# An attention backward kernel: dV and dK accumulated transposed with 512-column moving operands, and four turns per head given to the crossbar

## The chip, the cores and the metric

One core of a Trainium2 chip. The metric is the device time of one execution in microseconds, as the median of several runs. All runs used here were in the same, undisturbed state (one core has no second state to be confused with, and no run was more than 1.5% above the fastest of its kernel).

PE is TensorE (its weight loads are listed as PEld), DVE is VectorE, ACT is ScalarE, POOL is GpSimd, SP is SyncE. SP issues all the crossbar transposes, POOL issues the plain loads and stores of the attention.

## The reference, cut to what matters

The whole computation is a forward pass and its gradient. The part that the change touches is the gradient of 32 attention heads, each with S = 2048 queries and keys and a head size of 128:

```python
q = (x @ wq).reshape(B, Sq, H, Dh).transpose(0, 2, 1, 3)          # H = 32, Dh = 128, Sq = Sk = 2048
p = softmax(einsum("bhqd,bhkd->bhqk", q, k_cache) * Dh ** -0.5)
o = einsum("bhqk,bhkd->bhqd", p, v_cache)
...
# what jax.vjp asks for in each head, with dO the gradient of o:
#   dV = P^T dO          dP = dO V^T        dS = P * (dP - rowsum(P * dP)) * Dh ** -0.5
#   dK = dS^T Q          dQ = dS K
```

The weights' gradients and the gated branch come before and after this; the change does not touch them. All tensors are bf16.

## The kernel before

A matmul here contracts over the 128 partitions. `lhsT` is the loaded weight (128 columns at most), `rhs` is the moving operand (up to 512 columns), and the result goes to PSUM.

Each head has 16 "P slots" (scores, exponentials, transposed probabilities P^T, O) and then 16 "dS slots" (dP, dS, dS^T, dQ). One slot is one block of 128 queries. The slab of a slot, `Pq`, is 128 queries by 2048 keys, 512 KB; dS later overwrites P in it. The crossbar turns each slab, so there are 32 turns per head, and each is used five slots after it was asked for:

```python
skew = min(SKEW if fast else 2, NT // 2)      # SKEW = 5, NT = 16
def transpose_slab(hs, qt, name):             # P^T and dS^T, 512 KB each
    T = wpt.tile([P, NT, P], bf, name=name, tag="PT")          # a ring of 7 buffers
    nc.sync.dma_start_transpose(T[:], hs.slabs[qt][:])
    return T
def tail_part(hs, T, rhs, part):              # O from P^T and V, dQ from dS^T and K
    if part == 0:
        hs.acc = acc_tile()
    for kt in range(part * NT // 2, (part + 1) * NT // 2):
        nc.tensor.matmul(hs.acc[:, 0, :], lhsT=T[:, kt, :], rhs=rhs[:, kt, :], start=(kt == 0), stop=(kt == NT - 1))
```

The scores need K^T and dP needs V^T. Those were made by PE, 16 transposes of 128 columns each per head, with copies out of PSUM by ACT or DVE:

```python
def prep_kt(hs):
    KTv = hs.KT[:].rearrange("p (t q) -> p t q", q=P)
    pe_transpose_blocks(lambda j: hs.Kn[:, j, :], 0, NT, lambda g, n: KTv[:, g:g + n, :], "s")
def prep_vt(hs): ...                          # the same for V, copies by DVE
```

dV and dK were accumulated in their stored layout, in two halves of eight slabs each. Here the slab is the weight and dO or Q (128 columns) moves:

```python
class Partial:                                # [...] __init__ cut
    def step(self):
        kt = self.kt
        j = kt % 4
        if j == 0:
            self.tile = acc_tile()
        for qt in range(self.lo, self.hi):
            nc.tensor.matmul(self.tile[:, j, :], lhsT=self.slabs[qt][:, kt * P:(kt + 1) * P], rhs=self.rhs[:, qt, :],
                             start=(qt == self.lo), stop=(qt == self.hi - 1))
        self.kt += 1
        if j == 3 or self.kt == NT:
            # [...] first half: copy to the fp32 tile `part`; second half:
            fo_ = stg.tile([P, 4, P], bf, name="kvo", bufs=4)
            nc.vector.scalar_tensor_tensor(fo_[...], self.tile[...], self.factor, self.part[...], op0=ALU.mult, op1=ALU.add)
            nc.gpsimd.dma_start(self.out_dram.rearrange("(p t) d -> p t d", t=NT)[:, k0:kt + 1, :], fo_[:, :j + 1, :])   # 128 KB
```

A plan says in which slot each side task stands (b1 is the head's first P slot, b2 its first dS slot, pl the head before's first dS slot):

```python
for c in range(4):
    put(pl + q(c), 0, lambda c=c: load_k(hd(), c, 4))                # K in four loads of 128 KB
    put(pl + q(skew + 3 + c), 0, lambda c=c: load_v(hd(), c, 4))     # V too
put(pl + q(skew + 3), NT * P, lambda: prep_kt(hd()))
# [...]
put(b1 + q(NSC + 2), NT * P, lambda: prep_vt(hd()))
# [...]
spread(b1 + NTH, lambda: first("v", hd().dOn, 0, NTH, "v"))          # dV, first half
spread(b2, lambda: Partial(hd(), NTH, NT, hd().dOn, parts["v"], out_3[0, h], None))
spread(b2 + NTH, lambda: first("k", hd().Qn, 0, NTH, "s", SCALE))    # dK
spread(b2 + NT, lambda: Partial(hd(), NTH, NT, hd().Qn, parts["k"], out_2[0, h], None, SCALE))
```

## Time and profile before

| | before |
|---|---|
| time, median of 3 runs | 5019.34 us (5018.45 to 5020.46) |
| span of the profiled run, mean granted PE clock | 5024.2 us, 0.997 |
| attention (first scores to the last head's dQ and dK) | 3134 us, so about 98 us per head |

The page of the kernel before: the busy time of each engine with its share of the span, the granted PE clock and the busy share of the DMA engines in 40 slices (tenths), and the chain that ended last.

```profile
PE 4914.6 (98%) x53584; PEld 3475.1 (69%) x54480; DVE 2582.2 (51%) x6721; ACT 2575.9 (51%) x4637; POOL 961.8 (19%) x1507
...
PEclk9999999999999999999999999999999999999999
DMA  7887999999999999999999999999996665797876
...
PE 92%; DMA 3%; issue 3%; DVE 1%; ACT 0%; SPq 0%; POOL 0%; POOLq 0%; ACTq 0%; DVEq 0%
```

PE is the bound: it is busy nearly all the time, at full clock, and the chain is PE.

The costliest groups of the kernel before that the change touches: line, engine, operation, output and inputs, shapes, count, then busy us and the mean ns of one, then the idle time of PE just before them and what ended most of it. L737 is dV and dK, L677 is O and dQ, L146 is the transposes of K and V.

```profile
L737 PE MATMUL acc<-dOn,Pq 128*128 128x128 bf16 x8192 | 552.3, 219 | 10.1
L677 PE MATMUL acc<-Kn,dST 128*128 128x128 bf16 x8192 | 551.3, 219 | 9.1 <-DMA dST<-Pq 5.5
L677 PE MATMUL acc<-Vn,PT 128*128 128x128 bf16 x8192 | 547.4, 219 | 17.0 <-DMA PT<-Pq 10.1
...
L737 PE MATMUL acc<-Qn,Pq 128*128 128x128 bf16 x8192 | 540.6, 219 | 3.4
...
L146 PE MATMUL acct<-ident,Vn 128*128 128x128 bf16 x512 | 34.1, 219 | 0.0
L146 PE MATMUL acct<-ident,Kn 128*128 128x128 bf16 x496 | 32.7, 219 | 1.6
```

The mean of 219 ns is the length of one matmul in a pipeline where several overlap; what PE pays is the distance from start to start. The PE timeline shows it (start, length, line, tiles, count):

```profile
2005.03 1.50 PE L737 MATMUL acc<-dOn,Pq 128*128 128x128 bf16 x24
2006.37 0.59 PE L700 MATMUL dp<-VT,dOT 128*128 128x512 bf16 x2
2006.80 1.06 PE L677 MATMUL acc<-Kn,dST 128*128 128x128 bf16 x16
2007.70 0.59 PE L700 MATMUL dp<-VT,dOT 128*128 128x512 bf16 x2
```

Sixteen matmuls of 128 columns take 2007.70 − 2006.80 = 0.90 us to the start of the next group, so 56 ns each; two of 512 take 0.43 us, so 216 ns each. Taken over all starts, the pitches are 55.83 and 215.8 ns. This agrees with the Trainium skill, TensorE: Matmul & The Clock Gate, section "Back-to-back issue gap", whose formula, given there for an isolated matmul, comes to 55.8 and 215.8 ns. A matmul of 512 columns costs 3.87 of 128, not 4: that is all that wider moving operands can save.

Of some forms of 512 columns the trace before lacks records (4718 of 5376 in the attention are there, while the code asks for the full number), so counts of these are taken from the code, and PE's busy time before is somewhat too low.

Three stretches of the kernel before in the windows view (start and end in us, length, busy us and count of PE, PEld, DVE, ACT, POOL, then the granted PE clock, the DMA share, which counts overlapping packets and so can pass 1, and GB/s):

```profile
1000.00:3000.00 2000.00, 1978.28 (x25515) 1593.24 (x25924) 1282.88 (x3370) 1370.72 (x2294) 352.34 (x575) 1.00 1.09 210
2068.00:2088.00 20.00, 19.74 (x270) 16.44 (x273) 15.04 (x64) 15.19 (x28) 1.51 (x2) 1.00 1.25 234
2052.00:2062.00 10.00, 9.89 (x143) 8.47 (x142) 5.54 (x21) 7.77 (x15) 4.03 (x8) 1.00 1.05 173
```

PE is 98.9% busy at full clock in the long stretch.

### The profile page before, as it was taken

To read this page: it belongs to the slowest core of one execution; us is meant where nothing else is said; L and a number is where in the kernel's file an instruction comes from. 1 tells how busy PE (TensorE), PEld (TensorE's weight loads), DVE (VectorE), ACT (ScalarE), POOL (GpSimd) and SP (SyncE) were. 2 spreads that over 40 slices of the span, in tenths; PEclk is the share of its full clock that TensorE was granted. 3 is DMA by queue.
4 is the path that set the end of the run, shared out by engine and by line. 5 is a ranking of instruction groups with operands and counts; after the bars stand their busy time and mean duration, and the time that the engine had idled before them with its cause. 6 is when DMAs were issued, how large, how long until landed. Compare 5 with 4: busy or idle time off the path is not lost.

```text
span 5024.2 us, 128236 instructions
## 1 busy us (share of the span) xinstructions
PE 4914.6 (98%) x53584; PEld 3475.1 (69%) x54480; DVE 2582.2 (51%) x6721; ACT 2575.9 (51%) x4637; POOL 961.8 (19%) x1507
## 2 busy tenths in 40 slices
PE   9999999999999999999999999999889999999999
PEld 4445787787787788778778877877646666555554
DVE  4545666666666666666666666665425444200111
ACT  5422766766666676666667666666413333211000
POOL 3322111111111111111111111111222222211000
PEclk9999999999999999999999999999999999999999
DMA  7887999999999999999999999999996665797876
GB/s 260 273 206 167 211 213 205 206 215 212 202 214 216 201 212 208 214 208 209 215 202 213 206 213 210 209 215 203 209 196 206 195 189 183 223 264 178 171 140 121
DMA packets 2762803, 1031.39 MB, mean 205 GB/s; under 512 B 2665377, under 2 KB 2669602, under 8 KB 2762210
## 3 DMA queue, kind: packets, MB, share of 16 engines
q1 hardware_dynamic: 2659746, 699.38, 75.7%
q0 software_dynamic: 101856, 323.05, 20.0%
q8 instruction: 428, 7.01, 0.6%
q14 instruction: 165, 1.35, 0.1%
q10 hardware_dynamic: 608, 0.59, 0.0%
HBM read 175.31 MB, written 182.13 MB: 71 GB/s over the span
## 4 chain that ended last, share of the span: by engine, by line
PE 92%; DMA 3%; issue 3%; DVE 1%; ACT 0%; SPq 0%; POOL 0%; POOLq 0%; ACTq 0%; DVEq 0%
PE acc L737 18%; PE acc L677 18%; PE acc L975 13%; PE sp L630 8%; PE dp L700 7%; PE acc L1157 6%; PE acc L213 6%; PE u_ps L448 3%; PE g_ps L446 3%; PE dh L1036 3%; PE acc L531 3%; PE acct L146 2%; PE acc L945 2%; DMA dST<-Pq 1%; DMA xnT<-on_d 1%
## 5 line engine op out<-in xcount | busy, mean ns | idle before, releaser
L648 ACT ACTIVATE Pq<-sp 128x1024 bf16<-128x1024 f32 x1024 | 1048.1, 1024 | 309.7 <-PE sp L630 196.4
L737 PEld LDWEIGHTS <-Pq 128*128 128x128 bf16 x16384 | 1003.9, 98 | 244.3 <-issue 1.1
L703 DVE SCALAR_TENSOR_TENSOR Pq<-dp,negdelta,Pq 128x1024 bf16<-128x1024 f32 x512 | 655.3, 1280 | 37.7 <-PE acc L677 36.5
L706 ACT ACTIVATE t<-dp,negdelta 128x1024 bf16<-128x1024 f32 x512 | 568.1, 1116 | 178.4 <-PE dp L700 123.0
L677 PEld LDWEIGHTS <-PT 128*128 128x128 bf16 x8192 | 501.0, 98 | 128.6 <-DMA PT<-Pq 11.5
L677 PE MATMUL acc<-Vn,PT 128*128 128x128 bf16 x8192 | 547.4, 219 | 17.0 <-DMA PT<-Pq 10.1
L737 PE MATMUL acc<-dOn,Pq 128*128 128x128 bf16 x8192 | 552.3, 219 | 10.1
L677 PE MATMUL acc<-Kn,dST 128*128 128x128 bf16 x8192 | 551.3, 219 | 9.1 <-DMA dST<-Pq 5.5
L630 PE MATMUL sp<-KQ 128*128 128x512 bf16 x1762 | 547.1, 379 | 2.2 <-ACT Pq L648 2.1
L737 PE MATMUL acc<-Qn,Pq 128*128 128x128 bf16 x8192 | 540.6, 219 | 3.4
L700 PE MATMUL dp<-VT,dOT 128*128 128x512 bf16 x1728 | 540.8, 379 | 0.0
L707 DVE TENSOR_TENSOR Pq<-t,Pq 128x1024 bf16<-128x1024 bf16 x512 | 354.6, 693 | 359.7 <-ACT t L706 351.9
L677 PEld LDWEIGHTS <-dST 128*128 128x128 bf16 x8192 | 492.0, 98 | 68.2 <-DMA dST<-Pq 7.4
L718 ACT ACTIVATE dq_n<-acc,rsc 128x128 bf16<-128x128 f32 x512 | 188.4, 368 | 331.7 <-PE acc L677 329.4
L1174 DVE SCALAR_TENSOR_TENSOR junk<-acc,xn_all 128x512 f32<-128x512 f32 (+1 forms) x32 | 13.9, 453 | 635.6 <-ACT dxn L1173 635.6
L751 POOL DMA_DIRECT2D out_dram<-kvo x256 | 140.8, 550 | 999.7 <-DVE kvo L749 999.7
L671 POOL DMA_DIRECT2D on_d<-o_n x128 | 97.3, 760 | 721.4 <-DVE junk L689 374.8
L1038 DVE TENSOR_TENSOR du_blk<-dh,ah 128x256 bf16<-128x256 f32 x288 | 120.4, 419 | 195.5 <-PE dh L1036 193.4
L1173 ACT ACTIVATE dxn<-acc 128x512 f32<-128x512 f32 (+1 forms) x32 | 12.8, 407 | 396.7 <-PE acc L1157 389.2
L635 DVE TENSOR_REDUCE rs_all<-rsp 128x1 f32<-128x2 f32 x512 | 78.1, 153 | 255.7 <-ACT Pq L648 253.4
L50 DVE TENSOR_SCALAR o_n<-acc,rinv_all 128x128 bf16<-128x128 f32 x352 | 123.3, 350 | 161.5 <-PE acc L677 161.5
L648 ACT ACTIVATION_READ_ACCUMULATOR Pq<-sp 128x1 f32 x1024 | 200.5, 196 | 0.0
(213 smaller groups left out, 6977.0 us busy)
## 6 DMA issues: line engine op xcount, KB each, us to landing
out_dram<-kvo POOLq DMA_DIRECT2D x256, 128.0 KB, 4.2
ah<-a_d POOLq DMA_DIRECT2D x18, 1024.0 KB, 7.2
ah<-h_d POOLq DMA_DIRECT2D x18, 1024.0 KB, 9.4
du_d<-du_blk POOLq DMA_DIRECT2D x18, 1024.0 KB, 8.0
dg_d<-dg_blk POOLq DMA_DIRECT2D x18, 1024.0 KB, 9.7
h_d<-h_row POOLq DMA_DIRECT2D x64, 256.0 KB, 3.5
a_d<-a_row POOLq DMA_DIRECT2D x64, 256.0 KB, 3.7
x_all<-in_A_k_cache_dram SPq DMA_DIRECT2D x64, 256.0 KB, 3.8
```

What stands on the lines that cost most here:

```text
L213: nc.tensor.matmul(av[:, :CH], lhsT=w[:, i, :], rhs=srcT[:, i, cs], start=(i == 0), stop=(i == DT - 1))
L630: nc.tensor.matmul(sp[:, c * CH:(c + 1) * CH], lhsT=hs.QT[:, qt * P:(qt + 1) * P], rhs=hs.KT[:, hf * HW_ + c * CH: hf * HW_ + (c + 1) * CH ...
L648: nc.scalar.activation(Pq[:, hsl], sp[:], AF.Exp, scale=SCALE, accum_out=hs.rsp[:, hf:hf + 1])
L677: nc.tensor.matmul(hs.acc[:, 0, :], lhsT=T[:, kt, :], rhs=rhs[:, kt, :], start=(kt == 0), stop=(kt == NT - 1))
L700: nc.tensor.matmul(dp[:, c * CH:(c + 1) * CH], lhsT=hs.dOT[:, qt * P:(qt + 1) * P], rhs=hs.VT[:, hf * HW_ + c * CH: hf * HW_ + (c + 1) * C ...
L703: nc.vector.scalar_tensor_tensor(Pq[:, hsl], dp[:], hs.negdelta[:, qt:qt + 1], Pq[:, hsl], op0=ALU.add, op1=ALU.mult)
L706: nc.scalar.activation(t[:], dp[:], AF.Identity, bias=hs.negdelta[:, qt:qt + 1], scale=1.0)
L707: nc.vector.tensor_tensor(Pq[:, hsl], t[:], Pq[:, hsl], op=ALU.mult)
L718: nc.scalar.activation(hs.dq_n[:, qt % G4, :], hs.acc[:, 0, :], AF.Copy, scale=hs.rsc[:, qt:qt + 1])
L737: nc.tensor.matmul(self.tile[:, j, :], lhsT=self.slabs[qt][:, kt * P:(kt + 1) * P], rhs=self.rhs[:, qt, :], start=(qt == self.lo), stop=(q ...
L975: nc.tensor.matmul(accs[j][:, :nn], lhsT=lhs[:, st, cols], rhs=rhs[:, st, n0:n0 + nn], start=(st == 0), stop=(st == NT - 1))
L1157: nc.tensor.matmul(self.accs[sl][j][:, :nn], lhsT=ch[:, kk, sl * P:(sl + 1) * P], rhs=wT[:, k0 + kk, n0:n0 + nn], start=(self.k + kk == 0) ...
```

## The change

Intent: give dV and dK the cheaper form, with `nat` (dO or Q) as the weight and the slab moving, 512 columns at a time. The result is dV^T or dK^T, so it is written as bf16 into a tile that is free at that time (the head's K^T or V^T), turned by the crossbar, and stored in one transfer of 512 KB. And take the transposes of K and V off PE: the crossbar turns the loaded K and V.

```diff
+            def turn_nat(dst, src):
+                nc.sync.dma_start_transpose(dst[:].rearrange("p (t q) -> p t q", q=P), src[:].rearrange("p t d -> p (t d)"))
...
             class Partial:
                 def step(self):
-                    for qt in range(self.lo, self.hi):
-                        nc.tensor.matmul(self.tile[:, j, :], lhsT=self.slabs[qt][:, kt * P:(kt + 1) * P], rhs=self.rhs[:, qt, :],
+                    chunk, j = divmod(self.n, SUB)
+                    cs = slice(chunk * CH, (chunk + 1) * CH)                      # CH = 512, SUB = 4
+                    for qt in range(self.lo + m * j // SUB, self.lo + m * (j + 1) // SUB):
+                        nc.tensor.matmul(self.acc, lhsT=self.nat[:, qt, :], rhs=self.slabs[qt][:, cs],
                                          start=(qt == self.lo), stop=(qt == self.hi - 1))
...
-                            nc.gpsimd.dma_start(self.out_dram.rearrange("(p t) d -> p t d", t=NT)[:, k0:kt + 1, :], fo_[:, :j + 1, :])
+                    nc.vector.scalar_tensor_tensor(self.turned[:, cs], self.acc, self.factor, self.part[:, cs], op0=ALU.mult, op1=ALU.add)
+                    if chunk == NCH - 1:
+                        kvn = stg.tile([P, NT, P], bf, name="kvn", bufs=1)
+                        nc.sync.dma_start_transpose(kvn[:], self.turned)
+                        nc.gpsimd.dma_start(self.out_dram.rearrange("(p t) d -> p t d", t=NT), kvn[:])
...
-                    put(pl + q(skew + 3), NT * P, lambda: prep_kt(hd()))
+                    put(pl + q(NTH + 3), 0, lambda: turn_nat(hd().KT, hd().Kn))
...
-                put(b1 + q(NSC + 2), NT * P, lambda: prep_vt(hd()))
+                put(b1 + q(NTH + 3), 0, lambda: turn_nat(hd().VT, hd().Vn))
...
-                spread(b2, lambda: Partial(hd(), NTH, NT, hd().dOn, parts["v"], out_3[0, h], None))
+                spread(b2, lambda: Partial(hd(), NTH, NT, hd().dOn, parts["v"], hd().KT, out_3[0, h], None))
...
-                spread(b2 + NT, lambda: Partial(hd(), NTH, NT, hd().Qn, parts["k"], out_2[0, h], None, SCALE))
+                spread(b2 + NT, lambda: Partial(hd(), NTH, NT, hd().Qn, parts["k"], VT[:], out_2[0, h], None, SCALE))
```

Cuts are marked with dots. Turned K overwrites the K^T tile that dV^T stood in, so the K turn waits until the dV^T turn has read it; likewise V after dK^T.

## The prediction

> **What bounds the kernel now.** TensorE. The page gives PE busy 4914.6 us of 5024.2 (98%), and the chain of waits that ended last is 92% PE. The stretches view has PE 98.9% busy from 1000 to 3000 us (attention), clock 1.00. In the timeline, start to start I measure 55.8 ns for 128 columns and 215.8 ns for 512. Every one has its own weight load, so the loads (98 ns each) are hidden behind matmuls. The Trainium skill (TensorE: Matmul & The Clock Gate, "Back-to-back issue gap") gives N/2.4 + 2.5 ns, 55.8 and 215.8; the trace agrees, and disagrees with the 81 and 131 ns named beside it. So PE pays for columns, with about 2.5 ns per instruction.
>
> **Removed from PE.** dV and dK: 16384 matmuls of 128 columns become 4096 of 512 with the same columns. 16384 x 55.83 = 915 us against 4096 x 215.8 = 884 us: 31 us saved, no more. Transposes of K and V: 1008 matmuls x 55.8 = 56 us saved. Together 87 us, nearly all on the chain. Per head (98.2 us now) about 2.75 us.
>
> **Removed elsewhere, off the chain.** ScalarE's K^T copies (59.8 us), VectorE's V^T copies (43 us). 256 output stores of 128 KB become 64 of 512 KB.
>
> **Added.** 127 crossbar transposes of 512 KB on SP's one queue, about four per head beside 32. The DMA row reads nines, but that counts overlapping packets (the stretches view says 1.10). In bursts the queue moves about 1130 packets of 256 bytes per us, 1.8 us per transpose (290 GB/s; the skill's Advanced Engine Details and Errata, "X-Bar Transpose (TRN2)", expects 350 to 400); the mean is 665. 36 transposes per 95.5 us need 754 on average: it fits, with less slack.
>
> **The risk.** SP issues in order. The built order puts the output's turn after the 7th transpose of a half head and the K or V turn one later; the latter waits until the former has landed, since it overwrites what that reads. I estimate the next P^T or dS^T 2 to 3.5 us late. From landing to use they now have 4 to 5 us in the middle of the P^T half, more in the dS^T half after its middle. Mostly hidden, not always. The V and K loads around the 4th and 5th slot already leave 2 to 3 us (sometimes 0); these lose the 0.9 us which PE spent on the transposes, but the small output stores go away there.
>
> **Prediction.** 5019 - 87 + a few us of new waits per several heads: 4937 us (1.6% faster), 4915 to 4970 in eight of ten. Chances: faster by over 2% 0.12, within 2% 0.85, slower by over 2% 0.03.
>
> **What would show it.**
> - dV/dK matmuls: 4096, pitch 216 ns; PE busy about 4830 us; PE still about 98% busy in attention; weight loads down by about 13,300.
> - PE's waits on the DMAs of P^T and dS^T: now about 35 us in total; below 60 after. ScalarE and VectorE no new waits by PE.
>
> **What would make it wrong.** (a) The two extra transposes in a row stall PE over 1 us per half head: then P^T or dS^T waits exceed 60 us and the gain vanishes. (b) PE's slots of 2.65 us become 2.62, and ScalarE's 2.44 us of exponentials per slot (1024 + 196 ns, twice) or VectorE's 2.3 to 2.7 us in the first dS slots begins to bind. (c) Existing waits go too, as the small stores and copies did matter: then over 2% faster.

## More of the kernel before

PE's waits on the turned slabs, in the kernel before (total us, times, longest):

```profile
PE acc L677 <- DMA PT<-Pq: 10.1, 2, 7.5
...
PE acc L677 <- DMA dST<-Pq: 5.5, 6, 1.6
```

PE waited 15.6 us for late P^T and dS^T in the whole execution.

## The result, and the profile after

| | before | after |
|---|---|---|
| median (lowest to highest), 4 runs each | 5018.9 us (5015.51 to 5020.46) | 5169.22 us (5160.23 to 5171.77) |
| ratio, 95% interval | | 1.0297 (1.0279 to 1.0315) |
| span of the profiled run, mean granted PE clock | 5024.2 us, 0.997 | 5166.0 us, 0.984 |
| attention | 3134 us | 3278 us |
| the rest after the attention | 1407 us | 1405 us |

A ratio is the mean time of one kernel's fast runs over that of the other's of the same rounds, so not quite the ratio of the medians quoted beside it. The change is 3% slower, and all of it lies in the attention: +144 us there.

The page after, same rows as before (busy time of each engine, the chain that ended last):

```profile
PE 4941.3 (96%) x41184; PEld 2921.2 (57%) x41184; DVE 2542.5 (49%) x6657; ACT 2521.2 (49%) x4575; POOL 854.7 (17%) x1315
...
PE 85%; DMA 12%; issue 2%; DVE 1%; SPq 1%; ACT 0%; POOL 0%; POOLq 0%; ACTq 0%; DVEq 0%
```

Weight loads fell from 54480 to 41184, as intended. But DMA has grown from 3% to 12% of the chain.

The groups after that answer to those of before: dV, dK and dQ.

```profile
L681 PE MATMUL acc<-Kn,dST 128*128 128x128 bf16 x8192 | 568.6, 222 | 109.0 <-DMA dST<-Pq 108.8
...
L742 PE MATMUL acc<-Pq,dOn 128*128 128x512 bf16 x2048 | 535.3, 381 | 0.0
L742 PE MATMUL acc<-Pq,Qn 128*128 128x512 bf16 x2048 | 526.7, 380 | 0.0
```

The forms are as planned, 2048 + 2048 matmuls in place of 8192 + 8192, and nothing waits in front of them. The idle time is in front of dQ, whose lines did not change: 109.0 us where there were 9.1.

PE's waits on the turned slabs, after:

```profile
PE acc L681 <- DMA dST<-Pq: 108.8, 38, 12.7
PE acc L681 <- DMA PT<-Pq: 70.4, 41, 6.3
```

179.2 us in 79 waits, where before it was 15.6 us in 8.

**The account of the attention.** PE's work at full clock can be worked out from counts and pitches: before 34955 × 55.83 ns + 5376 × 215.8 ns = 3111.7 us, after 17563 × 55.83 ns + 9472 × 215.8 ns = 3024.6 us. So the change did take 87.1 us of work off PE. But the attention is 22 us longer than its work before and 253 us after. The waits for P^T and dS^T explain 164 us of this difference of 231. The clock explains most of the rest: the trace's clock record has PE at half clock for 10 us (one stretch) in the attention before and for 143 us after, in 26 stretches of 3.4 to 13.7 us. Not all of this time is worth counting, because in part of it PE stood idle anyway and the wait is already in the sum: 5 us before and 35 us after. Half of what remains is lost, ((143 − 35) − (10 − 5)) / 2 = 52 us. A third, small term is the start after a wait: idle time is counted from the end of a matmul, 219 ns after its start, while the next could have started after 56 ns, so each wait costs 0.16 us more than its idle time, about 12 us for 71 more waits. −87 + 164 + 52 + 12 = +141 us, against +144 measured.

**One such stall.** Three stretches of the trace after, seen through the windows view (columns as before):

```profile
1056.00:1066.00 10.00, 10.00 (x96) 6.46 (x94) 7.07 (x8) 6.56 (x11) 0.83 (x2) 1.00 1.14 245
1066.00:1076.00 10.00, 7.06 (x57) 3.97 (x55) 4.93 (x6) 4.96 (x7) 2.30 (x4) 1.00 1.22 151
1076.00:1084.00 8.00, 4.74 (x24) 2.82 (x25) 1.28 (x1) 0.37 (x1) 0.00 (x0) 0.63 1.13 262
```

In the middle stretch the DMA share is the highest of the three and the bytes moved are the fewest, 151 GB/s. In the third, PE is idle for a large part and its clock falls to 0.63.

What was in flight: the queue of SP (start, us until the issue was through, tiles) and then the issues of POOL (with what they waited for in brackets), both of the kernel after.

```profile
1060.23 3.12 SPq L755 DMA_TRANSPOSE kvn<-KQ  x1
1063.45 1.68 SPq L628 DMA_TRANSPOSE dST<-Pq  x1
1065.50 3.63 SPq L613 DMA_TRANSPOSE KQ<-Kn  x1
```

```profile
1065.93 0.54 POOL L756 DMA_DIRECT2D out_dram<-kvn  x1 [5.63 <-DMA kvn<-KQ]
1066.46 0.54 POOL L172 DMA_DIRECT2D wo_h<-in_A_wo_dram  x1
```

At 1060 us dV^T is turned (kvn from the shared tile), at 1065.5 K is turned. When the dV turn has landed, its 512 KB store starts, at 1065.93, beside the K turn and with small loads behind it. The K turn landed 11.86 us after its issue, by the DMA records. This is the longest of its 31; the median is 7.9 us, and 4.5 us in e1_no_store below, where the store is gone. The next dS^T, asked for behind it, came late, and PE stood:

```profile
1070.70 1.06 PE L681 MATMUL acc<-Kn,dST 128*128 128x128 bf16 x16
1071.60 0.59 PE L704 MATMUL dp<-VT,dOT 128*128 128x512 bf16 x2
1072.03 1.03 PE L742 MATMUL acc<-Pq,Qn 128*128 128x512 bf16 x4
1079.26 1.89 PE L681 MATMUL acc<-Kn,dST 128*128 128x128 bf16 x16 [6.21 <-DMA dST<-Pq]
1080.94 1.06 PE L704 MATMUL dp<-VT,dOT 128*128 128x512 bf16 x2
```

This is the PE timeline after: 6.21 us idle in front of dQ, and then its sixteen matmuls take 1080.94 − 1079.26 = 1.68 us to the start of the next group, where those at 1070.70 took 0.90: that is what half clock looks like in a row of starts. The Trainium skill, TensorE: Matmul & The Clock Gate, section "HAM oscillation — how this bites in real kernels", warns of idle gaps beyond about 3.4 us for this reason. The trace agrees as far as it goes: 20 of PE's idle gaps in the attention after are longer than that, against one before, and a stretch of half clock begins within 5.2 us of the start of each. But 3.4 us is no sharp limit here: the other six of the 26 stretches follow gaps of 2.1 to 3.4 us in the same way.

**Where the lateness arises.** Of the 179.2 us, 158.6 fall on the ninth P^T or dS^T of a half head, which is the first behind the K or V turn in SP's queue. And these transposes do not take longer once they are issued (median from issue to landing for dS^T: 5.3 us before, 4.8 after, where the landing is on record, 320 of 512); they are issued later. From the last write of a slab to the issue of its dS^T the median is 2.0 us before and 5.0 after, and for the ninth to twelfth of a head 2.9 and 10.7. So it is in SP's in-order queue that the delay is passed on.

### The profile page after: what moved, and what is told of

It reads as the page before. It is cut to its first block, busy times and chain, and to the rows that moved or that the text cites. A ratio compares the mean times of both kernels' runs of the same rounds, so it can differ in the third digit from the quotient of the medians.

```text
span 5166.0 us, 102151 instructions
## 1 busy us (share of the span) xinstructions
PE 4941.3 (96%) x41184; PEld 2921.2 (57%) x41184; DVE 2542.5 (49%) x6657; ACT 2521.2 (49%) x4575; POOL 854.7 (17%) x1315
## 4 chain that ended last, share of the span: by engine, by line
PE 85%; DMA 12%; issue 2%; DVE 1%; SPq 1%; ACT 0%; POOL 0%; POOLq 0%; ACTq 0%; DVEq 0%
PE acc L681 17%; PE acc L742 15%; PE acc L980 12%; PE dp L704 8%; PE sp L634 8%; PE acc L1162 6%; DMA dST<-Pq 5%; PE acc L213 5%; DMA PT<-Pq 4%; PE u_ps L448 3%; PE g_ps L446 3%; PE dh L1041 3%; PE acc L531 2%; PE acc L950 2%; PE acct L146 1%
## 5 line engine op out<-in xcount | busy, mean ns | idle before, releaser
L681 PE MATMUL acc<-Kn,dST 128*128 128x128 bf16 x8192 | 568.6, 222 | 109.0 <-DMA dST<-Pq 108.8
L681 PEld LDWEIGHTS <-dST 128*128 128x128 bf16 x8192 | 515.0, 99 | 263.7 <-DMA dST<-Pq 131.3
L704 PE MATMUL dp<-VT,dOT 128*128 128x512 bf16 x2048 | 620.5, 385 | 0.1
L634 PE MATMUL sp<-KQ 128*128 128x512 bf16 x2048 | 613.6, 382 | 2.3 <-ACT Pq L652 2.1
L742 PE MATMUL acc<-Pq,dOn 128*128 128x512 bf16 x2048 | 535.3, 381 | 0.0
L742 PE MATMUL acc<-Pq,Qn 128*128 128x512 bf16 x2048 | 526.7, 380 | 0.0
L742 PEld LDWEIGHTS <-Qn 128*128 128x128 bf16 x2048 | 201.1, 98 | 243.6 <-issue 6.1
L742 PEld LDWEIGHTS <-dOn 128*128 128x128 bf16 x2048 | 200.2, 98 | 238.3 <-issue 7.8
L634 PEld LDWEIGHTS <-KQ 128*128 128x128 bf16 x2048 | 180.4, 98 | 125.8 <-issue 5.9
L704 PEld LDWEIGHTS <-dOT 128*128 128x128 bf16 x2048 | 181.4, 99 | 120.7 <-issue 7.7
```

The costliest lines, as they stand in the source:

```text
L634: nc.tensor.matmul(sp[:, c * CH:(c + 1) * CH], lhsT=hs.QT[:, qt * P:(qt + 1) * P], rhs=hs.KT[:, hf * HW_ + c * CH: hf * HW_ + (c + 1) * CH ...
L704: nc.tensor.matmul(dp[:, c * CH:(c + 1) * CH], lhsT=hs.dOT[:, qt * P:(qt + 1) * P], rhs=hs.VT[:, hf * HW_ + c * CH: hf * HW_ + (c + 1) * C ...
L742: nc.tensor.matmul(self.acc, lhsT=self.nat[:, qt, :], rhs=self.slabs[qt][:, cs], start=(qt == self.lo), stop=(qt == self.hi - 1))
```

## The experiments

Theories at the start, for the 231 us:
- **Volume**: plain loads and stores and crossbar transposes share the same DMA engines, and four more transposes per head beside the plain traffic make P^T and dS^T late. The Trainium skill says as much of engines in DMA: Bandwidth & Descriptors, section "Issuing engines are not separate DMA queues": DMAs started by different engines run on the same 16 DMA engines and interleave. The trace agrees: in the stretch from 1066 us above, the transposes of SP's queue moved 83 GB/s beside 67 of POOL's, and in its two neighbours 231 and 245 beside 13 and 17.
- **Size**: the new 512 KB store is a block in the way, where four stores of 128 KB were not.
- **Order**: two turns in a row on SP's in-order queue, the second waiting for the first, delay what stands behind them, whatever else is in flight. This was the risk named in the prediction.
- **Place**: the turns stand in slots with little margin.

"before" in each row below is the kernel before, run on the same chip.

| run | before | this, median of 4 runs | ratio (95%) |
|---|---|---|---|
| e1_no_store (wrong results) | 5018.73 | 5021.84 | 0.999 (0.9969 to 1.0012) |
| e2_kv_only | 5018.73 | 5013.13 | 0.9985 (0.9968 to 1.0001) |
| e3_acc_only | 5018.73 | 5015.01 | 0.9987 (0.997 to 1.0003) |
| e4_chunks | 5018.73 | 5158.57 | 1.0289 (1.0263 to 1.0316) |
| d1_spare_tight | 5019.55 | 5095.86 | 1.017 (1.0119 to 1.022) |
| d2_spare_slack | 5019.55 | 5082.89 | 1.0125 (1.0105 to 1.0146) |
| e7_less_plain (wrong results) | 5019.55 | 4963.69 | 0.989 (0.9874 to 0.9907) |
| e8_kv_paced | 5019.55 | 4990.38 | 0.9933 (0.9916 to 0.9949) |
| g1_after_slow_loads | 5022.25 | 5207.65 | 1.0388 (1.0337 to 1.0439) |
| g2_kv_slow_loads | 5022.25 | 4967.6 | 0.9896 (0.9879 to 0.9912) |
| g3_after_all_slow | 5022.25 | 5175.14 | 1.0331 (1.0288 to 1.0374) |
| e5_before_big_store | 5022.25 | 5028.17 | 1.0013 (0.9996 to 1.0029) |
| d3_spare_less_plain (wrong results) | 5017.68 | 5032.48 | 1.0029 (1.0014 to 1.0043) |
| d4_before_less_plain (wrong results) | 5017.68 | 5006.91 | 0.9976 (0.9961 to 0.999) |
| d5_spare_plain | 5017.68 | 5197.7 | 1.0348 (1.0326 to 1.037) |

Where results are wrong it is on purpose. The others were correct. Several results missed what had been stated for them: e1, e7, d3 and e8 fell between the two ranges, e2 (by 3 us) and g1 above both, and d5 far above.

### e1_no_store: the kernel after, without the stores of dV and dK

```diff
-                        nc.gpsimd.dma_start(self.out_dram.rearrange("(p t) d -> p t d", t=NT), kvn[:])
```

> The changed kernel without the 64 stores of the turned dV and dK (512 KB each); those two outputs are wrong on purpose. All four extra crossbar transposes per head and SP's order stay. Theory 'store' (the 512 KB store slows the transposes in flight beside it): the PE stalls on P^T and dS^T (181 us of PE idle in the changed kernel) fall below 50 us, time 4915 to 4960. Theory 'order' (two extra transposes one slot apart on one in-order queue, the second waiting for the first to land): stalls stay, time 5120 to 5170.

Measured: 5021.84 us, 147 below the kernel after. All 36 transposes per head and their order are still there; 1 MB of stores per head is gone. The profiled run was the slowest of the four (5046.49 us) and still waited less than half as long, though not as little as before:

```profile
PE acc L681 <- DMA dST<-Pq: 68.7, 39, 4.0
...
PE acc L681 <- DMA PT<-Pq: 17.2, 18, 4.0
```

This lies between the two expectations, so neither theory is enough alone. The stores have a large part in it. Whether by their size or by their bytes is for the next run.

### e4_chunks: the kernel after, turned and stored in four pieces

```diff
-                    if chunk == NCH - 1:
-                        kvn = stg.tile([P, NT, P], bf, name="kvn", bufs=1)
-                        nc.sync.dma_start_transpose(kvn[:], self.turned)
-                        nc.gpsimd.dma_start(self.out_dram.rearrange("(p t) d -> p t d", t=NT), kvn[:])
+                    kvo = stg.tile([P, SUB, P], bf, name="kvo", bufs=4)
+                    nc.sync.dma_start_transpose(kvo[:], self.turned[:, cs])
+                    nc.gpsimd.dma_start(self.out_dram.rearrange("(p t) d -> p t d", t=NT)[:, chunk * SUB:(chunk + 1) * SUB, :], kvo[:])
```

> The changed kernel with dV and dK turned and stored in four pieces of 128 KB, each as soon as its 512 columns are there (two slots apart). Same bytes, more SP issues (10 per head instead of 4 beside 32). Theory 'store': spread small stores do no harm, as in the kernel before: 4930 to 4975. Theory 'order': more entries in the in-order queue, each waiting for VectorE: no better than 5100.

Measured: 5158.57 us, about as slow as the kernel after. The same bytes in pieces of 128 KB, spread over the half head, do not help. The run splits the turns as well, into ten issues per head in place of four, so it does not test the size of the store alone.

### e5_before_big_store: the kernel before, with one store of 512 KB

```diff
-                            fo_ = stg.tile([P, 4, P], bf, name="kvo", bufs=4)
+                            if k0 == 0:
+                                self.kvn = stg.tile([P, NT, P], bf, name="kvn", bufs=1)
...
-                            nc.gpsimd.dma_start(self.out_dram.rearrange("(p t) d -> p t d", t=NT)[:, k0:kt + 1, :], fo_[:, :j + 1, :])
+                            if self.kt == NT:
+                                nc.gpsimd.dma_start(self.out_dram.rearrange("(p t) d -> p t d", t=NT), self.kvn[:])
```

> The kernel before, with each head's dV and dK gathered in one tile and stored in one piece of 512 KB instead of four of 128 KB. If the size of the store by itself is harmful: over 5060. If it is harmful only beside extra transposes: 5010 to 5045.

Measured: 5028.17 us, ratio 1.0013, the same time. A large store where there are no extra transposes costs next to nothing. So the size by itself does no harm; for its part beside extra transposes there is e4_chunks alone, where small pieces gained nothing.

### e2_kv_only and e3_acc_only: each half of the change alone

e2_kv_only is the kernel before with the K and V turns of the change:

```diff
-                    put(pl + q(skew + 3), NT * P, lambda: prep_kt(hd()))
+                    put(pl + q(NTH + 3), 0, lambda: turn_nat(hd().KT, hd().Kn))
-                put(b1 + q(NSC + 2), NT * P, lambda: prep_vt(hd()))
+                put(b1 + q(NTH + 3), 0, lambda: turn_nat(hd().VT, hd().Vn))
```

e3_acc_only is the kernel after with these two lines undone in place (`prep_kt` and `prep_vt` at `q(NTH + 3)`).

> Only half of the change: K^T and V^T by crossbar, dV and dK as in the kernel before (16384 matmuls of 128 columns, 128 KB stores). Theory 'store': no 512 KB store, so only the 56 us of PE transposes go: 4955 to 4980. Theory 'order': a single extra transpose per half head costs at most a little: 4960 to 5010. Not decisive between them, but it says which half of the change does the harm: if over 5030, the crossbar turns of K and V alone do.

> The other half alone: dV and dK transposed, turned by crossbar and stored in 512 KB; K^T and V^T by PE as before. Expected without stalls: 5019 - 31 = 4988. Theory 'store': the store still meets the transposes of P^T and dS^T, so stalls stay: 5040 to 5150. Theory 'order': with no second transpose waiting behind the first, few stalls: 4985 to 5015.

Measured: 5013.13 and 5015.01 us. PE was given back 56 us in one and 31 us in the other, and 6 and 4 us of it arrive, neither clear of noise. Two transposes more per head eat nearly all of what they save; all of it together costs 237 us (the 87 saved and the 150 lost). The loss grows faster than the number of transposes, as it would where lateness comes through only after a margin is used up. The place differs too, though: in the trace of e2_kv_only the K and V turns stand behind the 15th P^T and the 15th dS^T, in the kernel after behind the eighth dS^T and the eighth P^T, next to the dV and dK turns. So e2_kv_only is not quite that half as it stands in the change.

### e7_less_plain: e1_no_store, and K and V loaded for the first two heads only

```diff
     def load_kv(hs, dst, cache, c, n):
+        if hs.h > 1:
+            return
```

> The changed kernel without the stores of dV and dK and with K and V loaded for the first two heads alone (wrong results on purpose): 2 MB of 3.4 MB of plain traffic per head gone, the transposes and PE's work as in the changed kernel. If plain traffic beside the transposes makes them late: stalls gone, 4925 to 4960. If the number or the place of the transposes alone does it: as without the stores, 5005 to 5050.

Measured: 4963.69 us, 58 below e1_no_store, and the waits are as they were in the kernel before:

```profile
PE acc L683 <- DMA PT<-Pq: 10.1, 7, 3.5
PE acc L683 <- DMA dST<-Pq: 8.4, 2, 5.4
```

All the transposes are still there, in the same order, with the V and K turns waiting for the dK and dV turns as in the change. So the order alone does not cost: it needs the plain traffic. It is not cleared as the path of the delay, since in the kernel after most of the waiting is right behind the turns. The attention of the profiled run is 3058.5 us, 76 below that of the kernel before (d4_before_less_plain below, with the same plain traffic taken from the kernel before, has 3135.4): here the saving on PE is nearly all there. The time as a whole shows less of it, because the part after the attention was 10 us longer in this run than in the kernel before.

### d1_spare_tight and d2_spare_slack: the kernel before with four useless transposes per head

```diff
+            def spare_turn(hs, qt):
+                if fast:
+                    T = stg.tile([P, NT, P], bf, name="spare", bufs=1)
+                    nc.sync.dma_start_transpose(T[:], hs.slabs[qt][:])
...
+                if qt in (7, 8):              # after that P^T; the same after dS^T
+                    spare_turn(hs, qt)
...
-                            fo_ = stg.tile([P, 4, P], bf, name="kvo", bufs=4)
+                            fo_ = stg.tile([P, 4, P], bf, name="kvo", bufs=3)
```

The last edit only makes room. d2_spare_slack has `(0, 2)` in the P slots and `(12, 14)` in the dS slots.

> The kernel before, its PE work untouched, with four spare crossbar transposes of 512 KB per head whose result nobody reads: a second transpose of the slab just turned, at the 7th and 8th slot of each half head, where the changed kernel has its extra ones. Theory 'place' (extra transposes hurt only where PE's slots are 2.65 us and P^T or dS^T has 4 to 5 us to spare): 5080 to 5200. Theory 'capacity' (36 transposes plus all other traffic per head is more than the DMA engines can do in time, wherever they stand): the same 5080 to 5200. If neither: within 20 us of 5019, and the harm must come from the waits that chain the turns in the changed kernel.

> The same four spare transposes per head, at slots 0 and 2 of the first and 12 and 14 of the second half, where slots take 3.9 us and the transposes have 8 to 14 us to spare. Theory 'place': within 20 us of 5019. Theory 'capacity': no better than the run with the spare ones at slots 7 and 8.

Measured: 5095.86 and 5082.89 us, so +76 and +63 (d1's spread is wide, 5083 to 5137, and its interval straddles 2%). PE's own work is that of the kernel before, nobody reads the spare tile, and yet PE waits (d1_spare_tight):

```profile
PE acc L684 <- DMA dST<-Pq: 39.6, 38, 2.7
...
PE acc L684 <- DMA PT<-Pq: 35.4, 26, 8.5
```

Four transposes per head, without anything else of the change, make the others late. In the totals the place mattered little, but the waits of d2_spare_slack say more:

```profile
PE acc L684 <- DMA PT<-Pq: 54.5, 36, 5.5
PE acc L684 <- DMA dST<-Pq: 7.3, 7, 4.3
```

The two spare transposes late in the dS half left dS^T nearly as it was (7.3 us against 5.5 in the kernel before). The harm is at the start of the P half: 44.6 of the 54.5 us fall on the fourth to sixth P^T, right behind the other two, where the loads of K run in this trace. So d2's places were not all as free as I took them to be, and place does matter.

### d3_spare_less_plain, d4_before_less_plain: the cross of transposes and plain traffic

d4 is the kernel before without the K and V loads of heads 2 to 31 and without the stores of dV and dK (2 MB per head in all); d3 is d1_spare_tight with the same taken away.

```diff
     def load_kv(hs, dst, cache, c, n):
+        if hs.h > 1:
+            return
...
-                            nc.gpsimd.dma_start(self.out_dram.rearrange("(p t) d -> p t d", t=NT)[:, k0:kt + 1, :], fo_[:, :j + 1, :])
```

> The kernel before with four spare transposes per head at slots 7 and 8 (5096 us with all its plain traffic), now without the stores of dV and dK and with K and V loaded for two heads alone (wrong results on purpose). If plain traffic and transposes hurt only together: the 76 us loss shrinks to under 25, 4990 to 5020. If the 36 transposes alone are too many for the queue: over 5050.

> The kernel before with the same 2 MB of plain traffic per head taken away and no spare transposes: the fourth corner. The stalls that were there (about 22 us in all of attention) at most go: 4995 to 5015 either way.

| median, us | with the plain traffic | without it |
|---|---|---|
| 32 transposes per head | 5019 | 5007 |
| 36 transposes per head | 5096 | 5032 |

Four transposes cost 77 us beside the plain traffic and 25 without it; the plain traffic costs 12 us beside 32 transposes and 64 beside 36. In the attention alone (one profiled run each) it is plainer still: 3134 and 3135 us in the upper row, 3213 and 3145 in the lower. Neither is dear by itself, both together are. The waits of d3_spare_less_plain:

```profile
PE acc L686 <- DMA PT<-Pq: 16.7, 8, 6.4
...
PE acc L686 <- DMA dST<-Pq: 3.3, 1, 3.3
```

20.0 us, against 75.0 in d1_spare_tight: most of what PE lost needed the two together. The cross does not say whether it is the mixture of two kinds that costs or the sum of the bytes, because d3_spare_less_plain moves no more per head than the kernel before (20.4 MB both, by the DMA records of 24 heads; d1_spare_tight 22.5).

### d5_spare_plain: four plain loads of 512 KB in place of the spare transposes

```diff
+            def spare_turn(hs, qt):
+                if fast:
+                    T = stg.tile([P, NT, P], bf, name="spare", bufs=1)
+                    nc.gpsimd.tensor_copy(T[0:1, 0, 0:1], hs.slabs[qt][0:1, 0:1])
+                    nc.gpsimd.dma_start(T[:], A_k_cache[0, hs.h].rearrange("(p t) d -> p t d", t=NT))
```

The copy of one element keeps the load from starting before that slab is there, so it stands where the spare transpose stood.

> The kernel before with four spare plain loads of 512 KB per head at about the slots where the spare transposes stood: the same bytes, but not through the crossbar and not on SP's queue. If the DMA engines are what is shared, these too make P^T and dS^T late: 5045 to 5110. If it is SP's queue of transposes: within 15 us of 5019.

Measured: 5197.7 us, +180, well outside what I expected, and the waits are of the same kind:

```profile
PE acc L685 <- DMA dST<-Pq: 71.2, 58, 3.9
PE acc L685 <- DMA PT<-Pq: 67.8, 44, 9.8
```

The same bytes as plain loads hurt the transposes more than transposes do (139.0 us of waits against 75.0; 22.5 MB per head in both). These loads do not pass through SP's queue, so nothing stands in order behind them there: what they share with P^T and dS^T is the DMA engines. Not separated: the one-element copies also make POOL wait for a slab, and its other issues stand behind that.

### e8_kv_paced and g2_kv_slow_loads: can half the change be placed well?

e8_kv_paced is e2_kv_only with the K turn held back, so that it stands after the 12th dS^T of the head before and not, as in e2_kv_only, after the 15th P^T of that head:

```diff
-            def turn_nat(dst, src):
+            def turn_nat(dst, src, after=None):
+                if after is not None:
+                    nc.vector.tensor_copy(dst[0:1, 0:1], after[0:1, S - 1:S])
...
+                    put(pl + q(NTH + 3), 0, lambda: turn_nat(hd().KT, hd().Kn, heads[h - 1].slabs[11]))
```

g2_kv_slow_loads adds that the four pieces of K and of V are loaded two slots apart, each held back by a one-element copy of a slab, where before they went out in a burst:

```diff
+            def load_slowly(hs, v, c, slab):
+                dst = hs.Vn if v else hs.Kn
+                nc.gpsimd.tensor_copy(dst[0:1, c * NT // 4, 0:1], slab[0:1, 0:1])
+                (load_v if v else load_k)(hs, c, 4)
...
-                        put(pl + q(c), 0, lambda c=c: load_k(hd(), c, 4))
-                        put(pl + q(skew + 3 + c), 0, lambda c=c: load_v(hd(), c, 4))
+                        put(pl - NT + 7 + 2 * c, 0, lambda c=c: load_slowly(new_head(h), 0, c, heads[h - 1].slabs[7 + 2 * c]))
+                        put(pl + 7 + 2 * c, 0, lambda c=c: load_slowly(hd(), 1, c, heads[h - 1].slabs[7 + 2 * c]))
```

> K^T and V^T by crossbar, dV and dK as in the kernel before, with the turn of K held back by a one-element copy so that it stands at slot 12 of the second half instead of slot 15 of the first. Theory 'place': most of the 56 us of PE time is gained, 4960 to 4985. Theory 'capacity': 5005 to 5020 like the version with the turn at slot 15.

> K^T and V^T by crossbar with the paced turn of K (4990 us), and the K and V loads two slots apart. Bursts: 4955 to 4980, the best version so far. Sum alone: 4985 to 4995.

Measured: 4990.38 and 4967.6 us, ratios 0.9933 and 0.9896. The 56 us which PE saves are nearly all there (5022.25 − 56 = 4966). PE's waits in g2_kv_slow_loads are 14.5 us, at the level of the kernel before:

```profile
PE acc L687 <- DMA PT<-Pq: 10.0, 4, 4.6
...
PE acc L687 <- DMA dST<-Pq: 4.5, 4, 1.9
```

This is the best correct version found; it beats both kernels.

Its mean load of the DMA engines is not lower than that of the kernel after. The stretch of 2000 us in the attention, g2_kv_slow_loads:

```profile
1000.00:3000.00 2000.00, 1976.25 (x25270) 1582.93 (x25686) 1279.09 (x3391) 1358.68 (x2297) 386.53 (x751) 1.00 1.17 224
```

and the kernel after:

```profile
1000.00:3000.00 2000.00, 1903.70 (x16676) 1186.82 (x16674) 1207.30 (x3217) 1282.40 (x2168) 274.06 (x436) 0.98 1.13 221
```

224 GB/s with PE busy 98.8% of the time, 221 GB/s with PE busy 95.2%. This does not clear the mean rate, because the rate after is that of a kernel that stalls. Per head it moves 22.5 MB, g2_kv_slow_loads 21.5; at the 95.5 us per head of the prediction, 22.5 MB would need 235 GB/s (an estimate from these two numbers), and no run here kept up more than 227 in this stretch. So for the whole change a limit of the mean rate is an untested rival. For the half it is not needed: e2_kv_only moves the same 21.5 MB per head, and from 5013 to 4990 to 4968 us only places and times differ (and the one-element copies that hold a transfer back).

### g1_after_slow_loads and g3_after_all_slow: the same pacing in the kernel after

g1 has the `load_slowly` of g2. g3 puts the K and V turns later as well:

```diff
-                    put(pl + q(NTH + 3), 0, lambda: turn_nat(hd().KT, hd().Kn))
+                    put(pl + q(NTH + 4), 0, lambda: turn_nat(hd().KT, hd().Kn, heads[h - 1].slabs[NTH + 4]))
...
-                put(b1 + q(NTH + 3), 0, lambda: turn_nat(hd().VT, hd().Vn))
+                put(b1 + q(NTH + 4), 0, lambda: turn_nat(hd().VT, hd().Vn, hd().slabs[NTH + 4]))
```

> The changed kernel, all its bytes and transposes, with the four 128 KB pieces of the next K and V no longer sent in one burst but two slots apart (each held back by a one-element copy of a slab). If bursts of plain traffic are what makes the turns late: 5060 to 5120 (the loads are half of the plain bursts, the 512 KB stores stay). If only the sum of DMA work counts: 5150 to 5180.

> As the changed kernel with slow loads, and the turns of K and V moved from right behind the turn of dV and dK to four to five slots later. If the neighbourhood of the two turns and the store mattered: 30 us or more below the run with slow loads alone. If not: within 15 us of it.

Measured: 5207.65 and 5175.14 us; g3 is 32 us below g1, which its expectation would read as an effect of the neighbourhood, but their intervals overlap, and neither beats the kernel after. The spread loads of g1 were put in slots 7 to 13, where in this kernel the turns and the big stores stand too; in its trace they go out behind the 7th to 11th transpose of a half, mostly one apart and not two, so the run does not space them as meant. In g3 the wait moved: PE now waits for K^T itself,

```profile
PE sp L640 <- DMA KQ<-Kn: 108.8, 30, 6.0
```

30 times in 32 heads: the later turn is too late for the next head's first scores. The pacing that saves half of the change does not save the whole, at least in these two forms.

## Why the prediction was wrong

Predicted was 4937 us (4915 to 4970), measured 5169.22.

- "PE pays for columns, with about 2.5 ns per instruction" and "Together 87 us": right. The counts in the kernel after, at the same pitches, give 87.1 us, e7_less_plain shows 76 of it in the attention, and g2_kv_slow_loads nearly all of its 56.
- "weight loads down by about 13,300" and 4096 matmuls: right (13,296; 2048 + 2048). No new waits of PE for ScalarE or VectorE: right (risk (b) did not come; 2.1 us for ScalarE before and after, 1.2 us for VectorE's scaling of Q and dO).
- **The step that failed is "The DMA row reads nines, but that counts overlapping packets" and "36 transposes per 95.5 us need 754 on average: it fits, with less slack".** It counted the transposes against the burst rate that transposes reach when they are nearly alone, and left out the plain loads and stores that run on the same DMA engines. The kernel's own trace before held a hint of it, in the stretches shown with its profile: 173 GB/s in a burst of loads against 234 GB/s where only transposes ran. The cross shows the missing term: four transposes cost 25 us without 2 MB of plain traffic per head and 77 with it. In the kernel after it did not fit: dS^T left SP's queue 5.0 us after its slab was ready (median), where before it was 2.0.
- From it followed "I estimate the next P^T or dS^T 2 to 3.5 us late … Mostly hidden, not always." With the stores beside it the K turn took 7.9 us to land (median; 11.86 in the stall shown above), without them 4.5. Measured waits of PE: 179.2 us where "below 60" stood. The "about 35 us" given there for the kernel before is more than PE's 15.6; it comes out if the waits of the weight loads on the same slabs, 18.9 us in that trace, are added.
- A term was absent altogether: what a long wait costs after it has ended. In the kernel after, all 20 idle gaps of more than 3.4 us and six shorter ones were followed by a time of half clock; 52 us of the loss came that way. Hence also, in part, "PE busy about 4830 us" against 4941.3: matmuls at half clock count as busy for longer, and the trace before lacks more records.
- The risk named in (a), that two turns in a row stall PE and the waits pass 60 us, is what the waits showed, and at the place that it named: 158.6 of the 179.2 us are right behind the turns. But two turns in a row are not enough: e7_less_plain keeps them and hardly stalls. What was wrong is the size: P^T was to come 2 to 3.5 us late, inside a margin of 4 to 5; at that place PE still waits 3.0 us on average, 53 times, when the margin is used up. And slower by over 2% was given a chance of 3%.

What is shown: PE's saving is real; the loss is late P^T and dS^T, plus the clock; most of it needs both the extra transposes and the plain traffic; and in the half change, place and time alone are worth 45 us (e2, e8, g2). What is argued: that in the whole change, too, the lateness comes through because several transfers coincide, so that it passes the 3 to 5 us between landing and use. The rival is that 22.5 MB per head is simply more than the DMA engines carry at PE's pace; no run here separates the two, and the pacing of g1 and g3 did not help. What is open: why a stretch of mixed traffic moves fewer bytes per us (151 against 245 and 262 GB/s in the stretches shown), and how much of d5_spare_plain's 180 us is POOL's order.

## What to carry to other kernels

Work moved from a busy engine to the DMA engines is paid in lateness: before you count on "it fits", add the plain loads and stores to the transposes, and read the rate from a stretch of the trace where both run; bytes per head over the time per head that you hope for, 235 GB/s here, is a quick test against the best rate that any run has kept up, 227. Then compare the margin between landing and use, slot by slot, with the longest delay seen there, and not with the mean; a long wait is paid again in clock (after all 20 gaps over 3.4 us in the kernel after). Where a change has two independent halves, run each alone and place the better one well: here half of the change, with its loads spread, gains 1%, and the whole loses 3%.

## What the Trainium skill lacked or had wrong

- Advanced Engine Details and Errata, "X-Bar Transpose (TRN2)", says that transposes are as fast as regular DMAs and expects 350 to 400 GB/s. The densest bursts in the trace before move about 1136 packets of 256 bytes per us, 290 GB/s, between that and the 261 GB/s that DMA: Bandwidth & Descriptors, "Latency and other measured facts", gives for one kernel with a non-contiguous middle dimension.
- None of the pages on DMA, TensorE and the errata says what transposes and plain DMAs cost each other. Here four transposes of 512 KB per head cost 77 us beside 2 MB of plain traffic and 25 us without it, and a mixed stretch moved 151 GB/s where its neighbours moved 245 and 262.
- DMA: Bandwidth & Descriptors, "Rules for kernel authors", says that a transpose next to ordinary DMAs needs nothing. The row is about wrong results, and there it held (d1_spare_tight, d2_spare_slack and d5_spare_plain are correct). It lacks a word on time: +180 us in d5_spare_plain.
- TensorE: Matmul & The Clock Gate, "Back-to-back issue gap", gives sustained spacings of 81 and 131 ns for 128 and 512 columns and keeps its formula for an isolated matmul. The trace has 55.8 and 215.8 ns in long streams of loads and matmuls; here the formula holds for the streams, and the two figures do not.
